# Weight conversion split between ScalarE and VectorE, and block 0's output product in three rounded passes, in a fused scan and feed-forward kernel

## The chip, the core and the metric

The kernel runs on one core of one Trainium2 chip. The metric is the time of one execution on the device, in microseconds; lower is better. Engines are named TensorE (PE in the rows, its weight loads PEld), VectorE (DVE), ScalarE (ACT), GpSimd (POOL) and SyncE (SP).

## What is computed

Three layers on 4 x 768 = 3072 tokens: a gated linear scan per head, a gated feed-forward layer, and a second feed-forward layer with a softmax gate.

```python
def _attn_ref(x, a, B, C):            # 4 batches, 8 heads, 768 steps, head 32, state 16
    for c in range(nc):
        L = np.exp(cum[:, :, :, None] - cum[:, :, None, :]) * causal
        M = np.einsum('bhin,bhjn->bhij', Cc, Bc) * L
        y[:, :, sl] = M @ xc + (Cc @ state) * decay_to_i
        state = decay_full * state + sum_j(Bc xc decay_from_j)
def _moe_ref(x, w_gate, w_val, w_out, rms_g):      # 256 -> 1536 -> 256
    xn = x / rms * rms_g
    g = xn @ w_gate
    return (g * sigmoid(g) * (xn @ w_val)) @ w_out
def _moe2_ref(x, w_in, w_out, g_ln):               # 256 -> 1024 -> 256
    h = x @ w_in
    solu = h * softmax(h)
    return (layernorm(solu) * g_ln) @ w_out
```

The weights come as 64-bit floats and are made into 32-bit floats on the chip.

## The kernel before

**Tiling.** The scan works in 24 units of 128 steps (four sequences of six chunks); four units make a block of 512 tokens, and there are six blocks. Unit u needs loads (`ld_bc`, `ld_xb`, `ld_cd`, `ld_L`), the exponentials of the decays on ScalarE, a mask on GpSimd (`at_lsel`), the product C B on TensorE (`at_cb`), its multiplication by the decays on VectorE (`at_mt`), the output product (`at_y`), the state (`at_s2`, `at_sbd`), the mean square on TensorE (`at_ms`, L415) and the normalised result as a rounded high part and a remainder (`at_xh`, `at_xl`).

**Rounded products.** A product of float32 operands is done in three passes on operands rounded for TensorE: high by high, low by high, high by low. The high half is a ScalarE copy, the low half a subtraction on VectorE or GpSimd. Block b then goes through 12 steps f of 128 columns: gate (`g_gate`, buffer pg) and value (`g_val`, pv) on TensorE, tanh on ScalarE, two multiplications on VectorE (`g_silu`, `g_mul`), rounding and remainder (`g_ah`, `g_al`), and the output product `o_mm` two steps later (LAG). Block 0 is different (WIDE = 1): its gated values stay plain float32 (tile aw, `g_mul`), and its output product takes them and the unrounded weights in one float32 product each, which is two instructions. Its first four steps are done in halves of 256 tokens and pairs of columns (`h_mm`, `oh_mm`), so that they can begin when two of the four units are there. The second layer follows per unit (`m_h`, softmax, a transposition through DRAM, `m_f`).

**Weight conversion.** The weights are 26 pieces of 512 x 128 numbers. `w_load` brings one as 64-bit words into a buffer. `w_conv` makes float32 of them by bits in three VectorE instructions: L136 shifts and masks the upper word, L139 merges its top two bits, L143 merges the top bits of the lower word. Then `w_hi` rounds on ScalarE and `w_lo` subtracts on VectorE or GpSimd. Pieces are numbered g0, v0, o0, g1, v1, o1 and so on for gate, value and output of the first layer (0 to 17), 18 to 21 for the second layer's input and 22 to 25 for its output.

**Order.** Every piece of work is an `op` with an engine, an assumed duration, a due time, the operations that it follows (`after`) and the buffers that it takes (`new`) and uses (`use`). `plan` simulates the engines: on each it takes, of the operations that could start within SLACK of the earliest, the one with the earliest due time. The result is a fixed order for each engine's queue. Due times come from the constants at the top: PRO (start of block 0), FIRST (its least length), PER (the time per unit of later blocks), Y0, YU, YO (attention units), HU, HO, HLAG, TAILGAP (second layer), LEAD and EARLY (weight loads). They set an order, not a time. GpSimd may take some of VectorE's operations (`alt`), and `lock` keeps the two from sharing what they share in the plan.

**Around the change.** From unit 4 to unit 10, one TensorE operation `at_ycb` holds the output product of unit u and the product C B of unit u+1.

Of the kernel before, what the change touches and what calls it, by code (L numbers as in the profile page):

```python
# [29 lines left out]
LEAD = 8.3  # L30
PER = (12.48, 1.18, 6.66)
WIDE = 1
PAIRS = 2
AHEAD = 4
PRO = 11.84
FIRST = 76.99
WARM = 7
Y0 = (2.78, 2.0)
YPOS = 0.52
YSPAN = 0.92  # L40
TAILGAP = 16.87
# [12 lines left out]
HU = (7.01, -17.89, -11.1, -8.79, 33.82, -5.71, 8.14, -4.61, -82.29, -12.62, -67.27, 34.26, 11.63, 9.92, 5.96, -9.59, 6.54, -76.96, -13.89, -23.49, 13.72, -1.73, -16.47, 14.72)
# [7 lines left out]
def fused_kernel(ctx, tc, aT, xbt, bcT, wg, wv, wo1, rg, wi2, wo2, gl, consts, out):  # L62
# [62 lines left out]
    def w_load(i):  # L125
        src = pieces[i][1]
        t = stg[i] = sp.tile([P, 1024], I32, name="stage", tag="u", bufs=BUFS["u"])
        S.dma_start(t.rearrange("p (k f) -> p k f", k=2), src.bitcast(I32).rearrange("(k p) f -> p k f", p=P))

    def w_conv(i, c):  # L130
        v = stg[i].rearrange("p (f w) -> p f w", w=2)
        if c == 0:
            wtm[i] = sp.tile([P, 512], I32, name="wt", tag="wt", bufs=BUFS["wt"])
        t = wtm[i]
        if c == 0:
            V.tensor_scalar(out=t, in0=v[:, :, 1], scalar1=3, scalar2=0x3FFFFFF8, op0=ALU.logical_shift_left,  # L136
                            op1=ALU.bitwise_and)
        elif c == 1:
            V.scalar_tensor_tensor(out=t, in0=v[:, :, 1], scalar=-0x40000000, in1=t, op0=ALU.bitwise_and,  # L139
                                   op1=ALU.bitwise_or)  # L140
        else:
            raw = w_raw(i) if pieces[i][0][0] == "o" else t
            V.scalar_tensor_tensor(out=raw, in0=v[:, :, 0], scalar=29, in1=t, op0=ALU.logical_shift_right,  # L143
                                   op1=ALU.bitwise_or)
# [548 lines left out]
    def oh_mm(f, m):  # L693
        h, j = divmod(f - HALF, PAIRS)
        if f == HALF:
            po[0, m] = pp.tile([P, 512], F32, name=f"po{m}")
        for q in range(2):
            T.matmul(po[0, m][:, 256 * h:256 * h + 256], w_raw(3 * j + 2).bitcast(F32)[:, 256 * q + m * P:256 * q + (m + 1) * P],
                     act[0, f]["aw"][:, 256 * q:256 * q + 256], start=(f == HALF and q == 0), stop=False, skip_group_check=True)
# [3 lines left out]
    def o_mm(b, f, m):  # L703
# [9 lines left out]
        for i, (aa, ww) in enumerate(() if b < WIDE else ((d["ah"], wo1_s[0]), (d["al"], wo1_s[0]), (d["ah"], wo1_s[1]))):  # L713
            T.matmul(po[b, m][:, :n], ww[:, f, m * P:(m + 1) * P], aa,  # L714
                     start=(f == 0 and i == 0), stop=(f == NF - 1 and i == 2))
# [54 lines left out]
    for i in range(26):  # L770
# [3 lines left out]
        for k in range(3):  # L774
            op(f"wc{i}.{k}", "DVE", 0.41 if k == 0 else 0.68, t, (w_conv, i, k),
               after=[f"wl{i}" if k == 0 else f"wc{i}.{k-1}"],
               new=[("wt", f"wt{i}")] if k == 0 else [], use=[f"st{i}", f"wt{i}"], lock=True)
# [5 lines left out]
        last = []  # L783
        if kind == "o":
            t = gdue(WIDE, 2 * c + LAG) - 8.0
# [16 lines left out]

    def at_ycb(u):
        at_y(u)
        at_cb(u + 1)


    for u in range(NU):
# [55 lines left out]
        cbop = f"cb{u}" if u <= blk[0][1] or u >= SPLIT else f"y{u-1}"  # L864
# [7 lines left out]
        op(f"y{u}", "PE", (1.13 if not s0 else 0.8) + (1.0 if yc else 0.0), Y, (at_ycb if yc else at_y, u),  # L872
# [384 lines left out]
```

## Time and profile before

| | |
|---|---|
| median of 3 runs | 535.02 us (534.51 to 536.44) |
| the profiled execution: its time | 534.42 us |
| the profiled execution: span, first to last instruction | 532.7 us |
| mean granted clock of TensorE, as a share of 2.4 GHz | 0.993 |
| busy: TensorE, its weight loads, VectorE, ScalarE, GpSimd | 98%, 81%, 78%, 58%, 22% |
| moved by DMA | 64.79 MB, 122 GB/s on average |

A busy TensorE is not one at its peak: the ends of matmuls are modelled and they overlap, so the distance between their starts is the better measure. A row of the timeline gives start, length, engine, line, operation, output and input, count, and in brackets the engine's idle time before it and what ended it. In a table of stretches each engine's busy time stands with its count of instructions, then the granted clock, the DMA engines' busy share and GB/s. A row of the groups by line gives count, total busy time, mean duration in ns, and the idle time before. Some instruction durations contain waiting for the memory port that VectorE and GpSimd share.

### The profile page before, as it was taken

How to read it: one execution, taken by the hardware profiler on the slowest of the kernel's cores; microseconds unless marked ns; L12 is line 12 of the kernel's file. 1: busy time of each engine (PE TensorE's matmuls, PEld its weight loads, DVE VectorE, ACT ScalarE, POOL GpSimd, SP SyncE). 2: the span in 40 equal slices, each digit the busy share in tenths (PEclk: the TensorE clock that was granted, in tenths of full speed). 3: DMA queues.
4: the chain of work that ended last, by engine and by line, in shares of the span. 5: the costliest groups of instructions: out<-in, count | busy, mean ns of one | idle time of the engine just before them, and what ended most of it. 6: DMA issues, size and time to landing. Idle time of an engine off the chain costs nothing.

```text
span 532.7 us, 9807 instructions
## 1 busy us (share of the span) xinstructions
PE 520.6 (98%) x3512; PEld 431.9 (81%) x3512; DVE 414.5 (78%) x757; ACT 306.5 (58%) x681; POOL 116.8 (22%) x144
## 2 busy tenths in 40 slices
PE   8799899999999999999999999999999999999997
PEld 8697666677888888888888888888888888888877
DVE  5889899999678989687887698569966767665484
ACT  6745454356538578475767867368744453444365
POOL 2523213102104152320124524013400010101001
PEclk9989899999999999999999999999999999999999
DMA  8764656242223345425367535343222221232100
GB/s 250 232 207 131 194 183 192 90 149 80 65 85 104 101 112 171 138 80 174 105 178 213 169 121 163 101 141 122 73 62 90 89 90 67 73 100 82 48 10 31
DMA packets 43249, 64.79 MB, mean 122 GB/s; under 512 B 7104, under 2 KB 29504, under 8 KB 43200
## 3 DMA queue, kind: packets, MB, share of 16 engines
q1 hardware_dynamic: 43056, 63.96, 38.9%
q8 instruction: 28, 0.46, 0.4%
q14 instruction: 21, 0.17, 0.1%
q10 hardware_dynamic: 144, 0.20, 0.1%
HBM read 50.31 MB, written 13.83 MB: 120 GB/s over the span
## 4 chain that ended last, share of the span: by engine, by line
PE 82%; DVE 13%; issue 2%; ACT 1%; DMA 1%; POOL 0%; SPq 0%; DVEq 0%; ACTq 0%; POOLq 0%
PE po L714 15%; PE pg L642 15%; PE pv L642 15%; PE pf L618 13%; PE ph L489 12%; DVE wt L139 2%; PE pcb L305 2%; PE y L380 2%; DVE wt L136 2%; PE y L375 2%; DVE th L672 1%; DVE wt L143 1%; DMA bc<-in_bcT_dram 1%; PE pcb L357 1%; DVE aw L679 1%
## 5 line engine op out<-in xcount | busy, mean ns | idle before, releaser
L685 ACT ACTIVATE ah<-th 128x512 fp32r<-128x512 f32 x60 | 37.8, 630 | 51.8 <-PE po L714 36.1
L668 ACT ACTIVATE th<-pg 128x512 f32<-128x512 f32 x72 | 42.7, 594 | 27.7 <-PE pg L642 24.3
L642 PE MATMUL pg<-xh,wg_h 128*128 128x512 f32 x136 | 57.3, 421 | 0.3 <-DVE th L672 0.2
L672 DVE SCALAR_TENSOR_TENSOR th<-th,pg 128x512 f32<-128x512 f32 x72 | 49.0, 680 | 10.9 <-ACT th L668 10.3
L642 PE MATMUL pv<-xh,wv_h 128*128 128x512 f32 x136 | 55.4, 407 | 0.0
L642 PE MATMUL pg<-xh,wg_l 128*128 128x512 f32 x136 | 53.8, 396 | 0.0
L642 PE MATMUL pg<-xl,wg_h 128*128 128x512 f32 x136 | 53.6, 394 | 0.0
L642 PE MATMUL pv<-xl,wv_h 128*128 128x512 f32 x136 | 53.4, 393 | 0.0
L642 PE MATMUL pv<-xh,wv_l 128*128 128x512 f32 x136 | 53.4, 392 | 0.0
L691 DVE TENSOR_TENSOR al<-th,ah 128x512 fp32r<-128x512 f32 x47 | 32.9, 700 | 25.1 <-ACT ah L685 24.8
L254 ACT ACTIVATE L<-L,cneg 128x128 f32<-128x128 f32 x160 | 50.1, 390 | 1.6 <-DMA L<-crow 1.6
L618 PE MATMUL pf<-wo_h,uth 128*128 128x256 f32 x176 | 49.9, 283 | 0.0
L618 PE MATMUL pf<-wo_h,utl 128*128 128x256 f32 x176 | 49.7, 282 | 0.0
L618 PE MATMUL pf<-wo_l,uth 128*128 128x256 f32 x176 | 49.5, 281 | 0.0
L714 PE MATMUL po<-ah,wo_h 128*128 128x512 f32 x120 | 49.5, 412 | 0.0
L679 DVE TENSOR_TENSOR th<-pv,th 128x512 f32<-128x512 f32 x60 | 41.5, 691 | 8.5 <-PE pv L642 4.1
L714 PE MATMUL po<-al,wo_h 128*128 128x512 f32 x120 | 47.3, 394 | 0.0
L714 PE MATMUL po<-ah,wo_l 128*128 128x512 f32 x120 | 47.3, 394 | 0.0
L554 POOL TENSOR_TENSOR sc<-sc,mhalf 128x1 f32<-128x1 f32 x24 | 13.6, 565 | 129.8 <-DVE sc L549 102.4
L258 POOL TENSOR_SCALAR_AFFINE_SELECT L<-L 128x1024 f32<-128x1024 f32 x20 | 23.6, 1179 | 79.8 <-ACT L L254 69.2
L489 PE MATMUL ph<-wi_h,xh 128*128 128x512 f32 x96 | 37.9, 395 | 0.0
L489 PE MATMUL ph<-wi_l,xh 128*128 128x512 f32 x96 | 37.5, 391 | 0.0
(165 smaller groups left out, 1296.7 us busy)
## 6 DMA issues: line engine op xcount, KB each, us to landing
L<-crow SPq DMA_DIRECT2D x20, 512.0 KB
scr<-dt SPq DMA_DIRECT2D x20, 512.0 KB
tt<-scr SPq DMA_DIRECT2D x80, 128.0 KB
bc<-in_bcT_dram SPq DMA_DIRECT2D x48, 128.0 KB
stage<-in_wo_dram SPq DMA_DIRECT2D x10, 512.0 KB
xb<-in_xbt_dram SPq DMA_DIRECT2D x24, 192.0 KB
stage<-in_wv_dram SPq DMA_DIRECT2D x6, 512.0 KB
stage<-in_wg_dram SPq DMA_DIRECT2D x6, 512.0 KB
```

What stands on the lines that cost most here:

```text
L254: A.activation(d["L"][:, h], d["L"][:, h], AF.Exp, bias=cneg[:, R(u) * 8 + h:R(u) * 8 + h + 1])
L258: G.affine_select(out=d["L"], in_=d["L"], pattern=[[0, 8], [1, P]], base=0, channel_multiplier=-1, compare_op=ALU.is_ge, fill=0.0)
L489: T.matmul(ph[c], xx[:, kk, k * P:(k + 1) * P], ww[:, kk, 512 * c:512 * c + 512], start=(i == 0), stop=(i == 5))
L554: G.tensor_tensor(out=sc[:, 7:8], in0=sc[:, 6:7], in1=mhalf, op=ALU.pow)
L618: T.matmul(d["pf"][:, 0:DM], uu[:, k], ww[:, k], start=(k == 0 and i == 0), stop=(k == 7 and i == 2))
L642: T.matmul(ps[:, :n], ww[:, kk, f * P:(f + 1) * P], xx[:, kk, :n], start=(i == 0), stop=(i == 5))
L668: A.activation(d["th"], d["pg"], AF.Tanh, scale=0.5)
L672: V.scalar_tensor_tensor(out=d["th"], in0=d["th"], scalar=1.0, in1=d["pg"], op0=ALU.add, op1=ALU.mult)
L679: V.tensor_tensor(out=out, in0=d["pv"], in1=d["th"], op=ALU.mult)
L685: A.activation(d["ah"], d["th"], AF.Copy)
L691: e.tensor_tensor(out=d["al"], in0=d["th"], in1=d["ah"].bitcast(F32), op=ALU.subtract)
L714: T.matmul(po[b, m][:, :n], ww[:, f, m * P:(m + 1) * P], aa, start=(f == 0 and i == 0), stop=(f == NF - 1 and i == 2))
```

## The change

- `w_load` loads a piece that PATH marks (19 of 26) from its fourth byte, so that rows are 2045 bytes instead of 2048 and the top byte of every number stands at the start of a 32-bit word, the lower mantissa bits in the word before. The buffer is declared in bytes.
- `w_conv` of a marked piece: two ScalarE instructions (parametric ReLU, one-byte input) in place of L136 and L139, then one VectorE merge. The others are converted as before.
- WIDE = 0: block 0's gated values are rounded (`g_ah`, `g_al`), and its output products are three passes on rounded weights, in the halved steps too. The output weights' rounding gets due times in block 0 and no longer follows block 0's output products.
- `at_ycb` is split: the product C B of unit u+1 is an operation `yb` of its own on TensorE, with a due time ahead of all others.
- All due times are new.

```diff
-PER = (12.48, 1.18, 6.66)
-WIDE = 1
+PER = (12.41, 0.68, 6.51)
+WIDE = 0
-PRO = 11.84
-FIRST = 76.99
+PRO = 24.77
+FIRST = 55.51
...
+PATH = (1, 1, 1, 1, 1, 1, 1, 1, 0, 1, 1, 1, 1, 1, 1, 1, 1, 0, 1, 0, 1, 0, 0, 1, 0, 0)
...
     def w_load(i):
         src = pieces[i][1]
-        t = stg[i] = sp.tile([P, 1024], I32, name="stage", tag="u", bufs=BUFS["u"])
-        S.dma_start(t.rearrange("p (k f) -> p k f", k=2), src.bitcast(I32).rearrange("(k p) f -> p k f", p=P))
+        t = stg[i] = sp.tile([P, 2, 2048], I8, name="stage", tag="u", bufs=BUFS["u"])
+        o = 3 * PATH[i]
+        S.dma_start(t[:, :, 0:2048 - o], src.bitcast(I8).rearrange("(k p) f -> p k f", p=P)[:, :, o:2048])
...
+        if PATH[i]:
+            if c == 0:
+                A.activation(t.bitcast(F32), stg[i].rearrange("p k (f w) -> p k f w", w=8)[:, :, :, 4], AF.Prelu,
+                             scale=-1.0, bias=-56.0, alpha=2.0 ** -35)
+            elif c == 1:
+                A.activation(t, t.bitcast(F32), AF.Prelu, scale=-2.0 ** 62, bias=-112.0 * 2.0 ** 27, alpha=2.0 ** -35)
+            else:
+                V.scalar_tensor_tensor(out=raw, in0=v[:, :, :, 0], scalar=5, in1=t, op0=ALU.logical_shift_right,
+                                       op1=ALU.bitwise_or)
...
         for q in range(2):
-            T.matmul(po[0, m][:, 256 * h:256 * h + 256], w_raw(3 * j + 2).bitcast(F32)[:, 256 * q + m * P:256 * q + (m + 1) * P],
-                     act[0, f]["aw"][:, 256 * q:256 * q + 256], start=(f == HALF and q == 0), stop=False, skip_group_check=True)
+            if WIDE:
...
+            else:
+                ops = [(ww[:, 2 * j + q, m * P:(m + 1) * P], aa) for aa, ww in ((d["ah"], wo1_s[0]), (d["al"], wo1_s[0]), (d["ah"], wo1_s[1]))]
+            for i, (ww, aa) in enumerate(ops):
+                T.matmul(po[0, m][:, 256 * h:256 * h + 256], ww, aa[:, 256 * q:256 * q + 256], start=(f == HALF and q == 0 and i == 0),
+                         stop=False, skip_group_check=True)
...
-            op(f"wc{i}.{k}", "DVE", 0.41 if k == 0 else 0.68, t, (w_conv, i, k),
+            onA = PATH[i] and k < 2
+            op(f"wc{i}.{k}", "ACT" if onA else "DVE", 0.64 if onA else 0.41 if k == 0 else 0.68, t, (w_conv, i, k),
...
-        op(f"w{i}", "DVE", 0.68, t, (w_lo, i, V), after=[f"wh{i}"] + last, use=wu, lock=True)
+        op(f"w{i}", "DVE", 0.68, t, (w_lo, i, V), after=[f"wh{i}"], use=wu, lock=True)
...
+        if yc:
+            op(f"yb{u}", "PE", 1.0, -1e6, (at_cb, u + 1), after=[f"y{u}", f"lbc{u+1}", f"ls{u+1}"], new=[("hc", f"pcb{u+1}")], use=[f"bc{u+1}", f"pcb{u+1}"])
```

## Rows read from the trace of the kernel before

**Rows 1.** The page, part 1: busy us, share of the span, instructions.
```profile
PE 520.6 (98%) x3512; PEld 431.9 (81%) x3512; DVE 414.5 (78%) x757; ACT 306.5 (58%) x681; POOL 116.8 (22%) x144
```
**Rows 2.** Table of stretches: before block 0, block 0, the rest, the end.
```profile
0.00:27.70 27.70, 23.37 (x261) 21.09 (x261) 20.07 (x39) 17.35 (x51) 11.66 (x20) 0.99 0.76 232
27.70:103.10 75.40, 72.21 (x524) 54.56 (x521) 69.98 (x125) 35.96 (x94) 20.24 (x19) 0.96 0.57 175
103.10:510.00 406.90, 406.65 (x2594) 339.40 (x2595) 310.34 (x549) 238.56 (x504) 82.68 (x101) 1.00 0.36 110
510.00:532.70 22.70, 18.34 (x140) 16.87 (x138) 14.09 (x46) 14.68 (x32) 2.19 (x4) 0.99 0.07 24
```
**Rows 3.** Chain of waits: whole span by engine; 60 to 124 us by line.
```profile
PE 82%; DVE 13%; issue 2%; ACT 1%; DMA 1%; POOL 0%; SPq 0%; DVEq 0%; ACTq 0%; POOLq 0%
...
by line: DVE wt L139 14.7%; DVE wt L136 10.7%; DVE th L672 10.6%; DVE wt L143 9.4%; issue 7.5%; DVE aw L679 7.4%; DVE th L679 4.3%; DVE al L691 3.8%; DVE wi_l L156 3.7%; DVE L L315 3.5%; PE pv L642 2.8%; DVE cd L267 2.4%; DVE xts L448 2.3%;
```
**Rows 4.** Timeline, 53 to 57 us.
```profile
53.72 0.42 DVE L136 TENSOR_SCALAR wt<-stage 128x512 int32<-128x512 int32 x1
...
55.51 0.27 DVE L396 SCALAR_TENSOR_TENSOR s<-s,e,y 128x64 f32<-128x64 f32 x1
...
55.82 0.63 ACT L444 ACTIVATE xts<-y,rgt 128x128 f32<-128x128 f32 x2 [2.47 <-DVE s L396]
...
56.50 0.61 PE L415 MATMUL y<-ones,sq 128*128 128x1 f32 x4 [1.46 <-ACT xts L444]
```
**Rows 5.** Table of stretches, columns as in group 2: clock in block 0.
```profile
20.00:40.00 20.00, 17.23 (x171) 15.69 (x171) 17.79 (x36) 9.00 (x24) 5.97 (x9) 0.91 0.72 220
50.00:70.00 20.00, 18.16 (x162) 13.80 (x154) 17.86 (x33) 7.73 (x20) 3.23 (x3) 0.91 0.50 147
```
**Rows 6.** Timeline, groups by line, and pieces of the chain: output products, and others.
```profile
100.34 2.74 PE L711 MATMUL po<-aw,wraw 128*128 128x512 f32 x6
...
L711 PE MATMUL po<-aw,wraw x32: 590/592/697, 66.0 to 106.6; 128*128 128x512 f32 x32
...
44.10 1.73 PE po L698 x8
...
132.99 1.40 PE po L714 x6
...
42.66 1.44 PE pv L653 x12
```
**Rows 7.** Groups by line: durations of rounding, tanh, scaled copy, remainder.
```profile
L152 ACT ACTIVATE wg_h<-wt 128x512 fp32r<-128x512 f32 x6 | 3.8, 633 | 5.8 <-DVE wt L143 5.8
L668 ACT ACTIVATE th<-pg 128x512 f32<-128x512 f32 x72 | 42.7, 594 | 27.7 <-PE pg L642 24.3 <-PE pg L653 3.1
L346 ACT ACTIVATE cb<-bc,cst 128x512 fp32r<-128x512 f32 x12 | 8.5, 712 | 0.0
L691 DVE TENSOR_TENSOR al<-th,ah 128x512 fp32r<-128x512 f32 x47 | 32.9, 700 | 25.1 <-ACT ah L685 24.8
L691 POOL TENSOR_TENSOR al<-th,ah 128x512 fp32r<-128x512 f32 x13 | 18.4, 1418 | 53.8 <-ACT ah L685 53.8
```
**Rows 8.** Table of stretches for L136 alone, then L139 alone: VectorE busy, block 0.
```profile
27.70:103.10 75.40, 10.52 (x17) 0.96 0.57 175
...
27.70:103.10 75.40, 14.02 (x17) 0.96 0.57 175
```
**Rows 9.** Waits, 0 to 103.1 us: total, times, longest.
```profile
ACT xts L444 <- DVE s L396: 8.1, 4, 2.5
```
**Rows 10.** Timeline: the two table loads of the execution.
```profile
1.23 1.28 ACT L1183 ACT_TABLE_LOAD   x1 [1.23 <-PEq L1246]
...
5.56 1.28 ACT L284 ACT_TABLE_LOAD   x1 [1.54 <-DVE cneg L1186]
```
**Rows 11.** Timeline of the sync queue: first and last of eight weight loads before 27.7 us.
```profile
1.25 0.41 SPq L128 DMA_DIRECT2D stage<-in_wo_dram  x1
...
22.06 0.38 SPq L128 DMA_DIRECT2D stage<-in_wg_dram  x1
```

More of the change, by code (lines that the diff above doesn't have):

```diff
@@ L132, in w_conv @@
         if c == 0:
             wtm[i] = sp.tile([P, 512], I32, name="wt", tag="wt", bufs=BUFS["wt"])
-        t = wtm[i]
-        if c == 0:
-            V.tensor_scalar(out=t, in0=v[:, :, 1], scalar1=3, scalar2=0x3FFFFFF8, op0=ALU.logical_shift_left,
+        t = wtm[i].rearrange("p (k f) -> p k f", k=2)
+        v = stg[i].bitcast(I32).rearrange("p k (f w) -> p k f w", w=2)
+        raw = w_raw(i) if c == 2 and pieces[i][0][0] == "o" else wtm[i]
+        raw = raw.rearrange("p (k f) -> p k f", k=2)
@@ L137, in w_conv @@
                             op1=ALU.bitwise_and)
         elif c == 1:
[L139 removed]
+            V.scalar_tensor_tensor(out=t, in0=v[:, :, :, 1], scalar=-0x40000000, in1=t, op0=ALU.bitwise_and,
                                    op1=ALU.bitwise_or)
         else:
[L142 to L143 removed]
+            V.scalar_tensor_tensor(out=raw, in0=v[:, :, :, 0], scalar=29, in1=t, op0=ALU.logical_shift_right,
@@ L714, in o_mm @@
             T.matmul(po[b, m][:, :n], ww[:, f, m * P:(m + 1) * P], aa,
-                     start=(f == 0 and i == 0), stop=(f == NF - 1 and i == 2))
+                     start=(f == 0 and i == 0), stop=(f == NF - 1 and i == 2), skip_group_check=(b == 0))
         if m == 1:
@@ L774, in fused_kernel @@
         for k in range(3):
-            op(f"wc{i}.{k}", "DVE", 0.41 if k == 0 else 0.68, t, (w_conv, i, k),
+            onA = PATH[i] and k < 2
+            op(f"wc{i}.{k}", "ACT" if onA else "DVE", 0.64 if onA else 0.41 if k == 0 else 0.68, t, (w_conv, i, k),
                after=[f"wl{i}" if k == 0 else f"wc{i}.{k-1}"],
-               new=[("wt", f"wt{i}")] if k == 0 else [], use=[f"st{i}", f"wt{i}"], lock=True)
+               new=[("wt", f"wt{i}")] if k == 0 else [], use=[f"st{i}", f"wt{i}"], lock=not onA)
         if kind == "p":
@@ L782, in fused_kernel @@
         wu = [f"wt{i}"]
-        last = []
         if kind == "o":
-            t = gdue(WIDE, 2 * c + LAG) - 8.0
+            t = gdue(WIDE, (2 * c if WIDE or c >= PAIRS else c) + LAG) - 8.0
             wu = [f"raw{c // 4}"]
@@ L897, in fused_kernel @@
         ready = [f"xl{u}" for u in range(u0, u0 + n)] if True else []
-        steps = list(range(NF)) if b >= WIDE else list(range(HALF, HALF + 2 * PAIRS)) + list(range(2 * PAIRS, NF))
+        steps = list(range(NF)) if b else list(range(HALF, HALF + 2 * PAIRS)) + list(range(2 * PAIRS, NF))
         for g, f in enumerate(steps):
@@ L929, in fused_kernel @@
             for m in range(2):
-                op(f"o{m}{s}", "PE", mm_us(N, 3) + 0.015, to, (o_mm, b, f, m), after=[f"al{s}"] + wo_n + ([f"o{m}{b}.{f-1}"] if f else []) + ([f"o0{s}"] if m else []),
-                   new=[(f"po{m}", f"po{m}{b}")] if f == 0 else [], use=[f"ah{s}", f"al{s}", f"po{m}{b}"])
+                op(f"o{m}{s}", "PE", mm_us(N, 3) + 0.015, to, (o_mm, b, f, m), after=[f"al{s}"] + wo_n + ([f"o{m}{prev}"] if g else []) + ([f"o0{s}"] if m else []),
+                   new=[(f"po{m}", f"po{m}{b}")] if g == 0 else [], use=[f"ah{s}", f"al{s}", f"po{m}{b}"])
         t = gdue(b, NF - 1) + LAG * 6 + 3
```

46 lines of the change are left out of this document (23 added, 23 removed).

## The prediction

> **What bounds the kernel now.** I read the page's busy shares first. TensorE is busy 98% of the span, VectorE 78%, ScalarE 58% [rows 1]. An average over stages says little, so the next view is the table of stretches, cut where block 0's first gate product starts (27.7 us) and where block 1's first starts (103.1 us) [rows 2]. The reader is to see three different stages. From 103.1 to 510 TensorE is busy 406.65 of 406.90 us: that stretch is TensorE's own work and nothing else. From 27.7 to 103.1, block 0, VectorE is busy 69.98 of 75.40 us (93%), while TensorE has 3.2 us idle and its granted clock is 0.96; ScalarE is busy only 35.96 us (48%). Before 27.7 no engine is full, and the DMA share is 0.76. So the stage to look at is block 0, and its scarce engine beside TensorE is VectorE.
>
> The chain of waits says the same: over the whole span 82% of it is TensorE, 13% VectorE, and the chain that ends at 124 us is mostly VectorE's from 60 us on; the first two instructions of the weight conversion (L136 and L139) are 25.4% of that view [rows 3]. One place shows the mechanism. At 53.7 us VectorE takes the three conversion instructions of one weight piece; L396, the small state update of an attention unit, comes behind them at 55.51, ScalarE's copy of that unit at 55.82, and TensorE's L415 at 56.50, after 1.46 us idle [rows 4]. The granted clock is 0.91 in 20 to 40 us and 0.91 in 50 to 70 us [rows 5]: parts of both stretches ran at the lower of the two levels, 1.2 GHz in place of 2.4 GHz, and what stands before the second is this gap. (0.09 + 0.09) x 20 = 3.6 us of full-speed work are lost there.
>
> **The change part by part.** *Block 0's output products.* Now each is a full float32 product in two instructions: 32 of 512 columns (L711) and 32 of 256 (L698). Six of L711 in a row take 2.74 us and one alone 0.592, so they start (2.74 - 0.592) / 5 = 0.430 us apart; eight of L698 take 1.73 us on the chain, 0.216 each [rows 6]. Together 32 x 0.430 + 32 x 0.216 = 20.7 us. After: 8 steps x 2 halves x 3 = 48 rounded products of 512 columns, 1.40 us for six in blocks 1 to 5, and 4 steps x 2 x 2 x 3 = 48 of 256 columns, 1.44 us for twelve [rows 6]: 48 x 0.233 + 48 x 0.120 = 16.9 us. **3.7 us** of TensorE's work go, in its own queue, with no cover in question.
>
> What pays for it: each of the 12 steps gains a rounding on ScalarE (0.633 us, as that of the weights) and a subtraction (0.700 us on VectorE, 1.418 on GpSimd) [rows 7]. The output product then starts 1.3 us later than its multiplication allows now. Two steps of lag, some 2 x 4.5 us, cover that, and blocks 1 to 5 already run this way without idle. The low halves of the output weights are needed in block 0 as well; they are computed there already, so only their order moves.
>
> *The conversion.* In the block 0 stage 17 pieces pass L136 and L139, 10.52 and 14.02 us [rows 8], so 1.44 us a piece: L136 takes 0.42 us where nothing disturbs it [rows 4], but 0.62 on average here. Four pieces are converted before 27.7 us, all marked in PATH, and by the order of the loads the 17 of the stage are 3 and 5 to 20; PATH leaves out 8, 17 and 19 of them, so 14 move, and one more (23) later. VectorE loses 14 x 1.44 = 20.2 us there and gains at most 12 x 0.700 = 8.4: 69.98 - 20.2 + 8.4 = 58.2 us. ScalarE gains 28 instructions. No parametric ReLU and no one-byte input is in the trace; the nearest rows are the rounding of the same shape, 0.633 us, and on either side the tanh from PSUM at 0.594 and the copy with a scale from SBUF at 0.712 [rows 7]. I take 0.633 (same shape, same memory) and keep the other two as ends. ScalarE: 35.96 + 28 x 0.633 + 12 x 0.633 = 61.3 us (60.2 to 63.5).
>
> By the Trainium skill ("ScalarE: Activation LUTs", Rules for kernel authors) a relu belongs on VectorE and not on ScalarE, which speaks against this part. Per piece the trace gives it little weight: 2 x 0.633 = 1.27 us against 1.44 on VectorE as it runs here; by the rule ScalarE would lose more than VectorE gains and the stage would not shrink.
>
> *What the stage then costs.* Three engines bound it. TensorE: 75.4 less 3.2 idle, less 3.0 for the clock (4% of 75.4), less 3.7 = 65.5 us. ScalarE: 61.3 us, and if it can be filled as VectorE was, to 93%, 65.9 us (68.3 with 0.712). VectorE: 58.2 / 0.93 = 62.6 us. The stage comes to 65.5 to 68.3; I take **67.0, so 8.4 us less**. That contains the 3.7 us of the products; the rest is idle time and half-clock time that I expect to go mostly.
>
> *The wait that is added.* VectorE's merge (L143's successor) waits for two ScalarE instructions, which stand behind tanh, squares and decay exponentials in ScalarE's order. Behind the merge on VectorE stand the unit's L396 and the mask products; ScalarE's L444, which TensorE's L415 follows, waited 8.1 us in four cases for L396 [rows 9]. If the pieces come too late, that gap stays, with ScalarE as its cause. Below nothing is not excluded: the same order may also bring L396 forward. I count it at 0, from -2 to +3 us.
>
> *Before 27.7 us.* VectorE loses 4 x 1.44 = 5.8 us of 20.07 [rows 2, 8], but ScalarE, whose tables are only loaded at 6.86 us [rows 10], has 17.35 us busy and gains 8 x 0.633 = 5.1; it is then nearly full from there on. I count 0, from -3 to +3.
>
> *Loads, the split, due times.* A converted piece is loaded from its fourth byte, rows of 2045 instead of 2048 bytes, with as many loads on the sync queue. I count 0; see the rivals. The attention product for the next unit becomes an operation of its own, with the same matmuls and first priority: 0. The new due times reorder everything; after 103.1 us there is 0.25 us of idle to win, and an order can only lose there: 0 to +3. The last 22.7 us have 4.4 us without TensorE: 0, from -2 to +2.
>
> The sum goes against the profiled execution: 532.7 - 8.4 = 524.3 us of span, plus 1.7 us outside it (534.42 - 532.7) = 526.0. The median of the runs is 0.6 above that execution: **526.6 us**.
>
> **The rivals.** *A, ScalarE takes VectorE's place.* Then the stage is filled less well, since squares, copies and roundings of the attention units stand behind the pieces in one queue. At 85% of ScalarE's time and 0.712 us an instruction it is 63.5 / 0.85 = 74.7 us, hardly a gain; with 0.633, 72.1. For it: ScalarE's load rises by 70% in one stage. Against: its idle time there is 39 us, and waits of the present order are VectorE's. Between the two, 2 us are won: 533 us.
>
> *B, a table load for each piece, slower.* ScalarE shows exactly two table loads, 1.28 us each, one ahead of the logarithm and one ahead of the first exponential; tanh, square and copy then run without any [rows 10]. If the parametric ReLU is not in the active set, each pair costs one load to it and one back: 14 x 2 x 1.28 = 35.8 us in the stage, and 61.3 + 35.8 = 97.1 us is more than the 75.4 it has. With 93% that is a stage of 104 us, and 8 x 1.28 = 10 us before it: about 570 us. It decides from 70.1 - 61.3 = 8.8 us on, seven loads in the stage. Against: copies, squares, exponentials and tanh share one set here, so simple functions seem to come with it. The Trainium skill ("ScalarE: Activation LUTs", Table sets: the hidden batching unit) says that each set carries the cheap functions as filler, relu among them, and does not name the parametric one; no run here shows it yet.
>
> *C, the odd rows load slowly.* Eight of these loads start before 27.7 us [rows 11], 8 x 0.524 = 4.2 MB of the 232 GB/s x 27.7 us = 6.4 MB moved there. If they took twice as long, the transfers' share would rise from 0.76 to 0.76 x 1.65 = 1.25, so the first gate product would come 0.25 x 27.7 = 7 us later; with the gain in the stage behind it, 534 us, no change.
>
> *D, more than forecast.* The stage falls to TensorE's 65.5, and of the 4.3 us that TensorE idles before 27.7 us [rows 2] some 3 go, with 2 at the end: 534.4 - 9.9 - 5 = 519.5 us.
>
> *E, the new order loses in the full stretch* what it wins in block 0, through a buffer that a later block waits for: 2% of 406.9 us is 8 us, so 535 us.
>
> **How the numbers follow.** Forecast 0.52 (521 to 531), A 0.18 (531 to 535), D 0.15, B 0.04, C 0.05, E 0.06. A measurement of this kernel can tell about 0.5% from no change, 2.7 us: faster means below 532.3. Faster: 0.52 + 0.15 + 0.06 of A = 0.73. Slower than 537.7: B, and 0.07 of A, C and E together = 0.11. The rest, 0.16, is no change. The range reaches from D with 2 us to spare to just above C and E: 517 to 536; it leaves out B, the far ends of A, C and E, and the best of D.
>
> **What would show it.** Right: ScalarE near 61 us in a block 0 stage of about 67 us, with instructions of 0.59 to 0.71 us and two table loads in all; VectorE under 85% there; TensorE's output products of block 0 adding up to 17 us; granted clock above 0.96 in that stage; the stretch behind still full. Wrong: table loads between the pieces (B); L415 waiting for ScalarE's queue with the same length of gap (A); the first gate product well after 28 us with the DMA share near 1 (C); idle TensorE behind block 0 (E).

## The result, and the profile after

| | before | after |
|---|---|---|
| median of the runs beside each other | 535.20 us (534.51 to 536.44, 4 runs) | 528.33 us (526.57 to 529.91, 4 runs) |
| profiled execution: time, span | 534.42, 532.7 us | 526.57, 524.8 us |
| mean granted clock of TensorE in it | 0.993 | 1.000 |

The ratio is 0.9871, with a 95% interval of 0.9846 to 0.9896: 6.9 us or 1.3% faster. The forecast was 526.6 us, 1.7 us less than measured; the measurement lies in its range and in its case. A repetition beside other runs gave 527.38 us (six runs).

Lines of the changed kernel are 13 or more below those of before: L136, L139 and L143 are L150, L153 and L156 for a piece that PATH leaves out, and L142, L145 (ScalarE) and L147 (VectorE) for a marked one; L396 is L409, L444 is L457, L415 is L428, L642 is L655, L672 is L685, and L711 and L698, the output products of block 0, are L733 and L717.

The page of after, busy time of each engine, and its chain by engine (before: [rows 1, 3]):

```profile
PE 514.3 (98%) x3544; PEld 434.0 (83%) x3544; DVE 391.8 (75%) x726; ACT 334.9 (64%) x731; POOL 126.2 (24%) x149
...
PE 84%; DVE 7%; ACT 5%; issue 1%; DMA 1%; POOL 0%; DVEq 0%; ACTq 0%; POOLq 0%; SPq 0%
```

VectorE lost 22.7 us and ScalarE gained 28.4. On the chain, VectorE's share fell from 13% to 7% and ScalarE's rose from 1% to 5%. The table of stretches, cut at the same events as [rows 2], block 0's and block 1's first gate product:

```profile
0.00:26.10 26.10, 23.47 (x236) 21.07 (x237) 11.47 (x27) 21.38 (x59) 9.88 (x20) 1.00 0.77 243
26.10:93.60 67.50, 65.12 (x575) 55.86 (x574) 60.41 (x108) 58.44 (x138) 29.59 (x29) 1.00 0.67 211
93.60:500.00 406.40, 405.40 (x2590) 338.74 (x2590) 304.08 (x542) 240.44 (x504) 84.53 (x97) 1.00 0.35 107
500.00:524.80 24.80, 20.30 (x149) 18.37 (x147) 15.84 (x52) 14.63 (x32) 2.19 (x4) 1.00 0.07 22
```

The reader is to see where the time went in these two executions, of which after's ran at full clock and before's at 0.993 (experiment 7 shows the change at 0.993). Block 0 takes 67.50 us instead of 75.40: 7.9 less. It starts 1.6 us earlier (26.10 for 27.70). Behind block 1's first gate product lie 524.8 - 93.6 = 431.2 us instead of 532.7 - 103.1 = 429.6: 1.6 us more. In the stage TensorE is now busy 96% of the time, VectorE 89% and ScalarE 87%; before it was 96%, 93% and 48%.

The ScalarE instructions of the conversion and the merge, as groups by line, and the table loads of the whole execution:

```profile
L142 ACT ACTIVATE wt<-stage 128x512 f32<-128x512 int8 x19 | 12.7, 670 | 0.2 <-POOL wv_l L169 0.2
L145 ACT ACTIVATE wt<-wt 128x512 int32<-128x512 f32 x19 | 12.1, 635 | 0.5
L147 DVE SCALAR_TENSOR_TENSOR wt<-stage,wt 128x512 int32<-128x512 int32 x15 | 11.5, 767 | 2.7 <-ACT wt L145 2.7
...
L1199 ACT ACT_TABLE_LOAD x1 | 1.3, 1283 | 1.2 <-PEq L1262 1.2
...
L1074 ACT ACT_TABLE_LOAD x1 | 1.3, 1283 | 0.0
```

There are two table loads in all, as before [rows 10]. The waits up to 93.6 us (engine, line, what it waited for: total, times, longest) answer [rows 9]:

```profile
DVE wt L147 <- ACT wt L145: 2.7, 1, 2.7
...
PE y L428 <- ACT xts L457: 1.8, 3, 1.1
...
ACT xts L457 <- DVE s L409: 0.3, 1, 0.3
```

The merge waited once for its ScalarE instructions, and TensorE's L428 waits 1.8 us in all for ScalarE's L457; before it waited 2.8 us for it (L415 for L444) and 2.3 us for VectorE's L394. L457 itself (L444 before) had waited 8.1 us for VectorE's small state update; of that 0.3 us are left, for L409.

### The profile page after: what moved, and what is told of

The parts are those of the page before. It is cut to its first block, busy times and chain, and to the rows that moved or that the text cites. A ratio compares the mean times of both kernels' runs of the same rounds, so it can differ in the third digit from the quotient of the medians.

```text
span 524.8 us, 9874 instructions
## 1 busy us (share of the span) xinstructions
PE 514.3 (98%) x3544; PEld 434.0 (83%) x3544; DVE 391.8 (75%) x726; ACT 334.9 (64%) x731; POOL 126.2 (24%) x149
## 4 chain that ended last, share of the span: by engine, by line
PE 84%; DVE 7%; ACT 5%; issue 1%; DMA 1%; POOL 0%; DVEq 0%; ACTq 0%; POOLq 0%; SPq 0%
PE po L733 17%; PE pg L655 17%; PE pv L655 16%; PE pf L631 13%; PE ph L502 12%; PE y L388 2%; PE y L393 1%; PE pcb L318 1%; ACT L L297 1%; PE pcb L370 1%; PE y L428 1%; PE wu L1197 1%; DVE th L685 1%; ACT wt L142 1%; DVE wraw L156 1%
## 5 line engine op out<-in xcount | busy, mean ns | idle before, releaser
L698 ACT ACTIVATE ah<-th 128x512 fp32r<-128x512 f32 x72 | 45.3, 629 | 44.6 <-PE po L733 32.4
L704 DVE TENSOR_TENSOR al<-th,ah 128x512 fp32r<-128x512 f32 x59 | 42.7, 723 | 24.7 <-ACT ah L698 23.9
L685 DVE SCALAR_TENSOR_TENSOR th<-th,pg 128x512 f32<-128x512 f32 x72 | 48.9, 679 | 14.2 <-ACT th L681 13.0
L692 DVE TENSOR_TENSOR th<-pv,th 128x512 f32<-128x512 f32 x72 | 49.7, 690 | 9.8 <-PE pv L655 4.1
L655 PE MATMUL pg<-xh,wg_h 128*128 128x512 f32 x136 | 55.9, 411 | 0.9 <-DVE th L685 0.9
L733 PE MATMUL po<-ah,wo_h 128*128 128x512 f32 x136 | 55.8, 410 | 0.0
L655 PE MATMUL pv<-xh,wv_h 128*128 128x512 f32 x136 | 54.4, 400 | 0.0
L733 PE MATMUL po<-al,wo_h 128*128 128x512 f32 x136 | 53.6, 394 | 0.0
L655 PE MATMUL pg<-xh,wg_l 128*128 128x512 f32 x136 | 53.6, 394 | 0.0
L733 PE MATMUL po<-ah,wo_l 128*128 128x512 f32 x136 | 53.5, 394 | 0.0
L655 PE MATMUL pg<-xl,wg_h 128*128 128x512 f32 x136 | 53.3, 392 | 0.0
L655 PE MATMUL pv<-xh,wv_l 128*128 128x512 f32 x136 | 53.2, 391 | 0.0
L655 PE MATMUL pv<-xl,wv_h 128*128 128x512 f32 x136 | 53.0, 390 | 0.0
L567 POOL TENSOR_TENSOR sc<-sc,mhalf 128x1 f32<-128x1 f32 x24 | 14.9, 622 | 136.3 <-DVE sc L562 136.1
L526 ACT ACTIVATE ut<-ph,sc 128x1024 f32<-128x1024 f32 x20 | 22.2, 1112 | 26.8 <-DVE sc L513 26.8
L513 DVE TENSOR_REDUCE sc<-ph 128x1 f32<-128x1024 f32 x20 | 24.4, 1221 | 19.5 <-PE ph L502 19.4
```

The costliest lines, as they stand in the source:

```text
L513: V.tensor_reduce(out=sc[:, 0:1], in_=ph[0], axis=AX.X, op=ALU.max, negate=True)
L526: A.activation(d["u"], ph[0], AF.Exp, bias=sc[:, 0:1], accum_out=sc[:, 1:2])
L655: T.matmul(ps[:, :n], ww[:, kk, f * P:(f + 1) * P], xx[:, kk, :n], start=(i == 0), stop=(i == 5))
L685: V.scalar_tensor_tensor(out=d["th"], in0=d["th"], scalar=1.0, in1=d["pg"], op0=ALU.add, op1=ALU.mult)
L692: V.tensor_tensor(out=out, in0=d["pv"], in1=d["th"], op=ALU.mult)
L698: A.activation(d["ah"], d["th"], AF.Copy)
```

## The experiments

Each kernel's time stands beside 9 to 19 runs of the kernel before on the same chip, whose medians were 535.25, 535.18 and 534.96 us. "Start" is block 0's first gate product, "stage" the time from it to block 1's, "rest" the time from there to the end of the span; these are of one profiled execution each. Before has 27.7, 75.4 and 429.6 us, after 26.1, 67.5 and 431.2.

**1. The kernel before without the work that moves.** In before's order the first two conversion instructions of the 19 marked pieces are left out, and the merge takes the upper word as it is:

```diff
+        if PATH[i] and c < 2:
+            return
```

> The kernel before in its own order, with the first two conversion instructions of the 19 pieces left out and nothing put in their place: the merge takes the upper word as it is, so the weights are wrong numbers; all other work is done. This is the relief of VectorE alone, without the price on ScalarE. Theory: the stage falls to TensorE's 69 us, 5 to 6 us won, 529 to 530 us; the difference to the run with the ReLUs in the same order is what ScalarE costs, 0 to 1.5 us. Rival 'VectorE was only busy, not binding': no change, 534 to 536.

527.32 us, ratio 0.9852 (0.9827 to 0.9877). The stage in the table of stretches:

```profile
27.56:96.48 68.92, 68.45 (x524) 53.57 (x521) 55.09 (x99) 36.35 (x94) 19.07 (x19) 0.98 0.58 191
```

And the chain of waits in the stage, by line, of this kernel (its lines are 7 below before's, so L718 is L711) and then of before:

```profile
by line: PE po L718 18.5%; PE pg L649 16.9%; PE pv L649 16.6%; PE po L705 10.3%; PE pg L660 10.2%; PE pcb L312 7.9%; PE pv L660 6.6%; PE y L382 3.3%; PE y L387 2.5%; PE y L422 2.5%; POOL wg_l L163 1.9%; PE y L392 0.8%; POOL r L440 0.7%; PE 
```

```profile
by line: DVE wt L139 11.0%; DVE wt L136 8.8%; issue 8.1%; DVE aw L679 7.2%; PE pv L653 6.0%; PE pg L653 5.8%; PE pg L642 5.1%; DVE th L672 5.0%; PE pv L642 4.8%; DVE L L315 4.6%; PE po L698 4.6%; DVE wt L143 4.1%; PE pcb L305 2.9%; DVE xts 
```

TensorE is busy 68.45 of 68.92 us, and no VectorE line stands among the large shares, where before had L139 and L136 at the top. So VectorE's two conversion instructions cost before 7.9 us, 6.5 of them in the stage, and without them TensorE alone bounds the stage. The time is 1.7 us below what I had expected. Leaving the instructions out also makes each piece ready earlier; experiment 2, where a piece passes three instructions again, loses at most 1.4 us of the stage by it. The first claim, that VectorE's load set the stage, is shown.

**2. The same work on ScalarE, in before's order.** `w_load` and `w_conv` as in the change; everything stands where before's plan put it, with the ScalarE instructions at the places of L136 and L139.

```diff
+PATH = (1, 1, 1, 1, 1, 1, 1, 1, 0, 1, ...)
...
+        if PATH[i]:
+            if c == 0:
+                A.activation(t.bitcast(F32), ..., AF.Prelu, scale=-1.0, bias=-56.0, alpha=2.0 ** -35)
```

> The kernel before, its order of instructions on every queue as it was, with the one part changed: for the 19 marked pieces the first two conversion instructions are the two parametric ReLUs on ScalarE, with the odd loads and the new merge; block 0's output product stays a full float32 product. My theory (VectorE's queue sets block 0's pace, TensorE's own work there would allow about 69 us of the 75.4): VectorE loses some 20 us of that stage and 4 to 6 us are won, 529 to 531 us. Rival 'the due times did it': no change, 534 to 536. Rival 'ScalarE takes VectorE's place': the merges wait behind exponentials and copies in an order made for something else, 536 to 540.

532.51 us, ratio 0.9937 (0.9913 to 0.9961). That is above the 529 to 531 us expected, and 5.2 us above experiment 1; I had expected at most 1.5 us between them. The table of stretches, up to block 0 and block 0:

```profile
0.00:31.36 31.36, 26.58 (x260) 22.96 (x261) 13.64 (x31) 21.58 (x59) 11.18 (x21) 0.87 0.68 205
31.36:101.72 70.36, 69.17 (x525) 53.27 (x521) 54.22 (x99) 50.83 (x122) 18.73 (x19) 0.99 0.58 186
```

The chain of waits up to block 0, by line:

```profile
by line: ACT L L297 20.1%; DMA stage<-in_wo_dram 12.4%; PE pcb L318 8.3%; ACT wt L145 7.3%; ACT wt L142 6.8%; PE y L393 6.5%; PE pc L1039 5.4%; PE y L428 5.2%; ACT xts L457 5.0%; ACT L297 4.1%; PE pv L289 3.2%; ACT sq L422 3.0%; issue 1.9%;
```

The price is paid before block 0, not in it. The start comes at 31.36 instead of 27.56 us, with the conversion's ScalarE instructions (14% of the chain there) between the exponentials L297 and the copies L457 for which TensorE waits. The stage loses only 1.4 us. A part of the price is clock: 0.87 up to block 0, where experiment 1 has 0.98. The two executions of this kernel with a mean clock of 0.995 and 0.997 took 530.48 and 530.83 us, still 3.2 and 3.5 us above experiment 1, whose four have 0.994 to 0.997.

**3. The change with the conversion back on VectorE**, in after's order:

```diff
-        o = 3 * PATH[i]
+        o = 0
...
-        if PATH[i]:
+        if False:
```

> The changed kernel in its own order, with only the conversion taken back: all pieces are loaded whole and converted by three VectorE instructions, issued at the places of the two ReLUs. Block 0's three passes, the split and the due times stay. Theory: VectorE's 60.4 us in the block 0 stage become 60.4 + 14 x 1.44 = 80.6, more than the stage's 67.5 us, so the stage is 81 to 86 us and the kernel 541 to 547 us. Rival 'the order alone did it': 528 to 531 us.

543.55 us, ratio 1.0137 (1.0099 to 1.0175); its stage:

```profile
29.74:111.63 81.89, 73.00 (x574) 60.17 (x573) 75.70 (x136) 42.79 (x110) 29.89 (x29) 0.92 0.54 173
```

VectorE is 92% busy, the 93% of before again: 75.70 / 0.93 = 81.4 us against 81.89. With the same order and the same products, the engine on which the conversion runs is worth 15 us. The Trainium skill ("ScalarE: Activation LUTs", Rules for kernel authors) puts a relu on VectorE. No relu was run on VectorE here; the conversion in VectorE's own instructions is slower than the two parametric ReLUs on ScalarE, with VectorE 92% busy in the stage.

**4. Two by two at the new due times.** The kernel before with the new constants (`due_only`), with the passes alone (`passes_newdue`), with the conversion alone (`conv_newdue`), each planned anew, and the change with all three:

```diff
-PRO = 11.84
-FIRST = 76.99
+PRO = 24.77
+FIRST = 55.51
...
+PATH = (0,) * 26
...
-WIDE = 0
+WIDE = 1
```

The first four lines stand for all due times and are `due_only`; the change with the `PATH` line is `passes_newdue`, and with the `WIDE` lines `conv_newdue`.

> The kernel before with only its due times and related constants replaced by the new ones, order planned anew. Theory: the due times have no gain of their own, since VectorE's work in block 0 stays; they were chosen for other operations: 534 to 541 us. Rival 'the due times carry the gain': 528 to 531 us.

> The changed kernel with no piece marked (PATH all 0), the order planned anew with the new due times for VectorE's three instructions: block 0's three passes, the split and the due times, without the ScalarE conversion. Theory: VectorE has the conversion's 20 us and the remainders' 8 us in one stage, some 80 us of work, which no order hides: 536 to 543 us, at or above the kernel before. Rival 'the passes and the due times carry the gain': 528 to 531 us.

> The changed kernel with block 0's output product back as one full float32 product on plain values (WIDE = 1), order planned anew with the new due times: the ScalarE conversion, the split and the due times, without the three passes. Theory: TensorE has 3.7 us more, VectorE 8 and ScalarE 7.6 us less, and TensorE holds the stage: 2 to 5 us more than the changed kernel, 530 to 533 us. Rival 'the passes bring nothing, since they cost ScalarE and VectorE what they save TensorE': 527 to 529 us.

| us (median), at the new due times | conversion on VectorE | on ScalarE |
|---|---|---|
| block 0 in float32 products | 551.76 | 531.43 |
| block 0 in three passes | 543.27 | 528.33 |

The ratios to before are 1.0321 (1.0285 to 1.0357) for `due_only`, 1.0145 (1.0110 to 1.0181) for `passes_newdue` and 0.9950 (0.9921 to 0.9979) for `conv_newdue`. The new due times alone cost 16.6 us; I had expected an order with a loss of at most 6. They start block 0 later and leave VectorE full, as the table of stretches of `due_only` shows:

```profile
0.00:34.80 34.80, 29.12 (x238) 25.40 (x238) 22.46 (x47) 18.30 (x52) 9.89 (x18) 0.75 0.66 207
34.80:115.23 80.43, 70.64 (x547) 53.21 (x547) 76.37 (x138) 40.01 (x105) 25.56 (x22) 1.00 0.55 181
```

VectorE is 95% busy in a stage of 80.43 us, and the stretch ahead of it is 7.1 us longer than before. In the table the conversion is worth 20.3 us with the one product and 14.9 with the other, the passes 8.5 and 3.1. The parts don't add. A likely reason is that these due times were chosen for all three parts together; no run has due times chosen for one part alone. Why the passes are worth as much as 8.5 us while VectorE is full isn't settled: each cell has an order of its own, and `due_only` is also the only one of the four without the split of `at_ycb`, so more than the passes or the conversion differs between its cell and its neighbours. The same table at the old due times was not run.

**5. How much room is left on each engine.** The change with one part enlarged at its place: a fourth pass in all of block 0's output products, of which the first lines show those of the halved steps (96 passes become 128: 16 x 0.233 + 16 x 0.120 = 5.6 us of TensorE), the first parametric ReLU twice, the merge twice.

```diff
-... for aa, ww in ((d["ah"], wo1_s[0]), (d["al"], wo1_s[0]), (d["ah"], wo1_s[1]))]
+... for aa, ww in ((d["ah"], wo1_s[0]), (d["al"], wo1_s[0]), (d["ah"], wo1_s[1]), (d["al"], wo1_s[1]))]
...
+                for _ in range(2):
                     A.activation(t.bitcast(F32), ..., AF.Prelu, scale=-1.0, bias=-56.0, alpha=2.0 ** -35)
...
+                for _ in range(2):
                     V.scalar_tensor_tensor(out=raw, in0=v[:, :, :, 0], scalar=5, in1=t, ...)
```

> The changed kernel in its own order, with a fourth rounded pass (remainder by remainder) in each of block 0's output products: 16 more products of 512 columns and 16 of 256, 16 x 0.233 + 16 x 0.120 = 5.6 us more of TensorE's work, and nothing else. It measures what the passes taken away were worth. Theory: the changed block 0 stage is held by TensorE's own work (65.1 of 67.5 us), so most of it shows: 4 to 6 us more than the changed kernel, 532 to 534 us. Rival 'ScalarE or VectorE holds it now': under 1.5 us more, 528 to 530.

> The changed kernel in its own order, with the first ReLU of each of the 19 pieces issued twice (the second writes the same numbers again): 14 x 0.667 = 9.3 us more on ScalarE in the block 0 stage and 3 us before it. If ScalarE has room (58.4 of 67.5 us busy there) and nothing urgent stands behind the pieces, under 1.5 us more than the changed kernel: 528 to 530 us. If ScalarE has become the bound (rival A of the prediction), all of it shows: 536 to 541. My theory lies between: before the stage ScalarE is nearly full (21.4 of 26.1 us) and the 3 us show there, in the stage part of the 9: 531 to 536 us.

> The changed kernel in its own order, with the merge of each of the 19 pieces issued twice on VectorE (the second writes the same numbers again): 14 x 0.69 = 9.7 us more on VectorE's 60.4 in a block 0 stage of 67.5 us, and 2.8 us before it on 11.5 of 26.1. It asks of VectorE what the doubled ReLU asked of ScalarE. Theory: VectorE has room before the stage (no later first gate product) and little in it: 3 to 6 us more than the changed kernel, 531 to 534. If VectorE is free: 528 to 530; if it is still as tight as ScalarE proved: 538 to 541.

| | time, us | above 528.33 | work added |
|---|---|---|---|
| four_passes | 530.75 | 2.4 | 5.6 TensorE |
| extra_act | 539.96 | 11.6 | 12.9 ScalarE |
| extra_dve | 542.09 | 13.8 | 13.3 VectorE |

The ratios are 0.9911 (0.9878 to 0.9944), 1.0068 (1.0043 to 1.0092) and 1.0118 (1.0083 to 1.0153). The work added on ScalarE and VectorE is the difference of the group's busy time (25.6 - 12.7, and 22.0 + 5.7 - 11.5 - 2.9 for the merges). From the tables of stretches, first the stage of `four_passes`:

```profile
27.15:98.83 71.68, 69.86 (x604) 60.22 (x604) 60.66 (x111) 59.89 (x142) 29.92 (x29) 1.00 0.61 198
```

Then `extra_act`, up to block 0 and block 0:

```profile
0.00:31.03 31.03, 25.89 (x236) 23.19 (x237) 12.23 (x27) 24.73 (x64) 10.65 (x20) 0.85 0.66 211
31.03:104.49 73.46, 68.25 (x573) 57.10 (x574) 59.97 (x107) 66.05 (x151) 29.34 (x28) 0.97 0.60 191
```

And the stage of `extra_dve`:

```profile
29.28:103.46 74.18, 67.43 (x574) 56.82 (x573) 68.52 (x120) 58.77 (x138) 28.96 (x29) 0.98 0.61 190
```

I expected ScalarE and VectorE to take half of such an addition or more into their idle time. They took next to none: 1 us more on either is about 1 us more of the kernel, part of it ahead of the stage (the start of `extra_act` is at 31.03), and part of it by the clock, which is 0.974 to 0.990 in the executions of the two kernels and 0.994 to 1.000 in those behind 528.33 us. The fuller engine ends at 90% of the longer stage (ScalarE, 66.05 of 73.46) and at 92% (VectorE, 68.52 of 74.18). TensorE, which looks the fullest at 96%, has more room than these two, but how much is not settled: of 5.6 us added, 2.4 show in the medians, uncertain by about 2, and 4.2 in the stage of the two profiled executions, both at full clock there (71.68 for 67.50 us). All three expectations were missed, the first by 1.3 us on the low side, the others by 4.0 and 8.1 us on the high side; for ScalarE rival A's 536 to 541 came true.

**6. Some of the start's conversion on VectorE.** VectorE is busy only 11.47 of the first 26.1 us, ScalarE 21.38. In after's order, pieces 0 to 3, and in a second kernel 0 and 3 alone, are loaded whole and converted on VectorE:

```diff
+ONA = tuple(0 if i in (0, 1, 2, 3) else p for i, p in enumerate(PATH))
...
-        if PATH[i]:
+        if ONA[i]:
```

> The changed kernel in its own order, with pieces 0 to 3, the four that are converted before block 0 starts, loaded whole and converted by VectorE at the places of the ReLUs. ScalarE loses 8 x 0.65 = 5.2 of its 21.4 us there, VectorE gains 4 x 1.1 = 4.4 on 11.5 of 26.1. Theory (ScalarE's queue is full from 8.4 us to the first gate product and sets it): the first gate product 2 to 4 us earlier, 525 to 527 us, better than both kernels. Rival 'TensorE's own work (23.5 of 26.1 us) or the chain of the attention units sets the start': no change, 527.5 to 529.5. Rival 'VectorE's new instructions stand ahead of the units' products': slower, 530 to 533.

> As the run before, with only pieces 0 and 3 (the gate pieces) on VectorE: ScalarE loses 2.6 us before block 0. Theory: half of the effect of four pieces, 526 to 528 us; no change, 527.5 to 529.5, if ScalarE's queue does not set the start.

530.54 us (0.9919, 0.9892 to 0.9945) and 527.56 us (0.9859, 0.9830 to 0.9889): the one slower than the change, the other not distinguishable from it. With four pieces the start came at 31.56 us. That stretch, in the table of stretches (the kernel's lines are 1 below after's):

```profile
0.00:31.56 31.56, 27.75 (x237) 24.37 (x237) 16.30 (x35) 17.73 (x52) 10.76 (x20) 0.87 0.66 207
```

A wait of ScalarE in it (total, times, longest), where before has 0.7 us for the same pair of lines (L409 for L394) and after none worth a row:

```profile
ACT sq L423 <- DVE s L408: 7.5, 2, 5.4
```

TensorE's gap there, in the timeline of `start_on_dve`, and the same place in that of after:

```profile
20.46 0.61 PE L429 MATMUL y<-ones,sq 128*128 128x1 f32 x4 [1.95 <-ACT xts L458]
```

```profile
18.40 0.61 PE L428 MATMUL y<-ones,sq 128*128 128x1 f32 x4 [0.50 <-ACT xts L457]
```

The idle engine had no use for the work at that place: the conversion now stood ahead of the unit's L408 in VectorE's queue, ScalarE waited up to 5.4 us for it, and TensorE behind ScalarE (1.95 us here, 0.50 in after). The theory, a start 2 to 4 us earlier, failed; the rival with the units' products named the mechanism and the time. No version that was run and does the whole work is clearly faster than the change.

**7. The change once more**, unaltered, for the spread of its runs:

> The changed kernel once more, unchanged, beside the runs below: 527 to 530 us. Its profiled execution so far had the full clock all through (1.00) and 524.8 us of span, its other executions 0.994 to 0.996 and 526.6 to 528.2. If the difference is the clock, an execution with one stretch of 3.4 us at the lower level is 1.7 us longer, with two 3.4 us longer, and the stretches lie before or in block 0, where TensorE has gaps, not behind it.

527.38 us (525.03 to 529.29), ratio 0.9850 (0.9820 to 0.9880). By the mean granted clock of an execution, from this series and the first, and before in the last two series:

| clock | after, us | before, us |
|---|---|---|
| 0.999 to 1.000 | 525.03, 525.16, 526.57, 526.57 | 533.31 to 533.71 (6 runs) |
| 0.996, 0.997 | 528.20, 528.29, 528.33, 528.36 | 533.61, 533.93 |
| 0.992 to 0.994 | 529.29, 529.91 | 533.92 to 535.42 (12 runs) |
| 0.986 to 0.990 | | 535.74 to 536.58 (10 runs) |

The profiled execution of this series has 0.993. Its table of stretches, up to block 0 and block 0:

```profile
0.00:25.02 25.02, 22.00 (x237) 19.54 (x237) 11.49 (x27) 21.39 (x59) 10.02 (x20) 1.00 0.78 248
25.02:96.26 71.24, 67.57 (x574) 58.66 (x574) 60.26 (x108) 58.84 (x138) 28.94 (x29) 0.95 0.63 201
```

It starts block 0 1.1 us earlier than the first execution of after and takes 3.7 us longer for it; the rest is 431.2 us in both. From 20 to 40 us, the table of stretches of this execution, and of the first one of after:

```profile
20.00:40.00 20.00, 16.59 (x150) 15.17 (x149) 12.79 (x29) 15.93 (x37) 9.05 (x11) 0.83 0.77 245
```

```profile
20.00:40.00 20.00, 17.87 (x181) 16.07 (x180) 16.26 (x36) 19.55 (x51) 10.38 (x13) 1.00 0.81 264
```

One place in the timelines of the two, in the same order:

```profile
32.49 1.01 PE L428 MATMUL y<-ones,sq 128*128 128x1 f32 x4 [2.56 <-DVE th L692]
```

```profile
32.22 0.61 PE L428 MATMUL y<-ones,sq 128*128 128x1 f32 x4 [1.05 <-ACT xts L457]
```

The same program has this gap with 2.56 us in one execution and 1.05 us in another. Behind the longer one a part ran at 1.2 GHz: four matmuls of L428 take 1.01 us instead of 0.61, and 17% of the stretch's clock is gone. Behind the shorter one 2.4 GHz stayed. So at before's own mean clock of 0.993 the change brings 4.2 us in the stage (75.40 to 71.24), and 7.9 only at full clock, which four of its ten executions had.

## Why the prediction was right, and where its sizes were off

**The bound was read rightly.** Three experiments hold the claim that VectorE's queue ended block 0: leaving its first two conversion instructions out gains 7.9 us (1), putting them back costs 15 (3), and the fill of 93% taken from before gives the stage of 3 within 0.5 us.

**The stage: 67.5 us against 67.0, in the execution at full clock.** Its terms held there within 3 us each; TensorE is busy 65.1 us, with 65.5 forecast. The parametric ReLU was taken at 0.633 us from the rounding; it measured 0.670 and 0.635. ScalarE came to 58.4 us (61.3 forecast) and VectorE to 60.4 (58.2), mainly because its 17 last conversion instructions there take 14.7 us, where before 16 took 11.8. At 89% VectorE is above the 85% that was named as a sign of being right. Output products: before's 62 of L711 and L698 in the stage are busy 14.41 + 7.94 = 22.35 us, after's 90 of L733 and L717 there 11.14 + 6.62 = 17.76. Scaled to all 64 and all 96 (two of L711 at 0.48, six of L733 at 0.265) that is 23.3 and 19.4 us, so some 4.0 less; 3.7 were forecast, from distances of starts (16.9 us after) and not from busy time. A part of this is probably clock, which was 0.96 in before's stage.

**What the passes bring** was put at their full 3.7 us. That they show in full is not what experiment 5 says: of 5.6 us more on TensorE 2.4 showed in the medians, and 3.8 at full clock (529.09 and 530.33, mean 529.7, against 525.9 as the median of the four in the table above). In the stage by itself 4.2 showed. By these shares 3.7 us are worth 1.6 to 2.8. Experiment 4 gives 3.1 in the medians and 4.5 at full clock (the four executions of `conv_newdue` at 0.999 or more have a median of 530.4), with another order. So whether this term was too large stays open. For the relief of VectorE the sum left 4.7 of the 8.4 us; without a price on ScalarE it is 6.5 in the stage of experiment 1.

**The clock is the term that missed the median.** I counted 3.6 us of full-speed work as lost in before, took 3.0 us off TensorE's stage for it, expecting that this "half-clock time" would go mostly, and put the median 0.6 us above the profiled execution. The table of experiment 7 shows that before gains little at full clock: about 533.5 us instead of 534.7 at 0.993 (the middles of the two cells), so 1.2 us. In after the same loss of clock goes with more: 529.6 at 0.993 (two executions) against 525.9 at full clock, 3.7 us. So the change is worth 7.6 us at full clock and 5.1 at 0.993. Probably TensorE waited for VectorE in before, so that a slower TensorE only waited less, while in after the engines are nearly level; no run separates this from the gap itself, which was 1.5 us longer in the execution at 0.993 (2.56 for 1.05). The execution that was profiled ran at full clock throughout and had 526.57 us, against a sum of 526.0; the median execution did not, and lies 1.8 us above it. So the step that failed is the clock: the half-clock time went in four of ten executions only, and the 0.6 us between the profiled execution and the median, taken over from before, became 1.8. That the execution which was profiled is one of the four, and so agrees with the sum within 0.6 us, is partly luck.

**Start and rest were counted at 0** with bounds of 3 us, and came to -1.6 and +1.6; that they cancel is luck, and the start of the second profiled execution is another 1.1 us earlier. Part of the rest is one gap just behind block 1's start. Here VectorE's queue, the wait that ends last, and TensorE:

```profile
95.39 1.13 POOL L271 TENSOR_SCALAR_AFFINE_SELECT L<-L 128x1024 f32<-128x1024 f32 x1 [3.79 <-issue]
...
95.60 1.46 DVE L156 SCALAR_TENSOR_TENSOR wt<-stage,wt 128x512 int32<-128x512 int32 x1
...
96.99 0.68 DVE L169 TENSOR_TENSOR wi_l<-wt,wi_h 128x512 fp32r<-128x512 f32 x1
...
97.59 0.67 DVE L685 SCALAR_TENSOR_TENSOR th<-th,pg 128x512 f32<-128x512 f32 x1
...
98.32 0.50 PE L655 MATMUL pg<-xh,wg_h 128*128 128x512 f32 x1 [0.94 <-DVE th L685]
```

It is a piece that PATH leaves out: its last instruction on VectorE, L156, takes 1.46 us beside a GpSimd instruction, where L153 just ahead of it took 0.69 without one. L685 stands behind it, and TensorE goes on at 98.32, where its last start was at 96.99 and its starts are 0.23 us apart: 1.1 us lost. The other 0.5 us weren't located. It is a loss behind block 0, as in rival E, at a fifth of its price, but through VectorE's queue and not through a buffer. In all kernels with before's order the rest is 428.8 to 429.6 us, with the new due times 430.3 to 433.3.

**The rivals.** *A, ScalarE takes VectorE's place*, didn't decide the change, but experiments 2 and 5 show its mechanism: in an order not made for it the work on ScalarE gives back 5.2 of 7.9 us, and in after's own order the next microsecond on it costs one. What spoke against A, 39 us of idle time, was the wrong measure, since the forecast used most of it up; the better one is the fill, where 58.4 us stand against some 90% of 67.5. *B* is out: two table loads for 38 parametric ReLUs among exponentials, tanh and copies. The trace agrees with the Trainium skill ("ScalarE: Activation LUTs", Table sets: the hidden batching unit) for the copies, which it names among the cheap functions of every set, and shows the same for the parametric ReLU, in the set that is active here. *C* is out: with rows of 2045 bytes the DMA share before block 0 is 0.77 at 243 GB/s, it was 0.76 at 232, and the start is earlier. *D* came in its smaller part: the start is 1.6 and 2.7 us earlier in the two profiled executions, where D has 3, but the stage stayed above 65.5, and the best execution, 525.0 us at full clock, is far from 519.5.

**The added wait** was 0, as taken: L147 waited once, 2.7 us, and the gaps of L428 fell. The split of `at_ycb` was counted at 0 and not run by itself: in TensorE's queue all seven products C B stand directly behind their output product, as they did before.

## What to carry to other kernels

Work may be moved off a full engine onto an idle one even where a single instruction is hardly faster there, but most of the gain may hang on the order and on the other parts: here the same moved work gave 2.7 us in the old order and 3.8 in an order planned anew with the new due times, the new due times without it lost 16.6, and all parts together gave 6.9. Idle time summed over a stage is no reserve; an engine at 87% to 90% of a stage may have none left, which doubling one of its instructions shows in one run. A change can make the time depend more on the clock, as here (3.7 us for 0.7% of the mean clock, 1.2 before), so forecast the median from the spread of the clock and not from one execution.

## What the hardware showed that was not expected

Reading one byte in eight and writing 32-bit integers cost ScalarE almost nothing: 0.670 and 0.635 us at 128x512, beside 0.636 for the rounding L165 of the same shape.

The granted clock before block 0 fell behind a wait of TensorE in several kernels, but the length of one gap doesn't tell whether it falls. Here the gap ahead of the same four matmuls at 18 to 21 us, the wait for L457 (L458), stands beside the mean clock up to block 0:

| kernel | that gap, us | mean clock up to block 0 |
|---|---|---|
| four_passes | none listed | 0.94 |
| extra_dve | none listed | 0.88 |
| after | 0.50 | 1.00 |
| start2_on_dve | 1.12 | 1.00 |
| conv_in_old_order | 1.13 | 0.87 |
| conv_back_in_new_order | 1.95 | 0.94 |
| start_on_dve | 1.95 | 0.87 |
| extra_act | 2.04 | 0.85 |

The rows of `start2_on_dve` and `conv_in_old_order`, and one of `four_passes`:

```profile
19.30 0.61 PE L429 MATMUL y<-ones,sq 128*128 128x1 f32 x4 [1.12 <-ACT xts L458]
```

```profile
20.38 0.61 PE L428 MATMUL y<-ones,sq 128*128 128x1 f32 x4 [1.13 <-ACT xts L457]
```

```profile
12.16 2.22 PE L318 MATMUL pcb<-bc 16*128 16x128 f32 x32 [1.40 <-DMA bc<-in_bcT_dram]
```

The same length of gap came once with full clock and once with 4 us of full-speed work lost (0.13 x 31 us). In `four_passes` and `extra_dve` the clock fell earlier, between 14 and 16 us, behind waits of 1.40 and 1.01 us for a load at 12 us that after does not have; `conv_back_in_new_order` has one of 1.12 us there and kept the full clock until 22 us. In after a gap of 1.05 us at 32 us cost no clock. What decides between these isn't shown.
